# Loading wq in eight row-strided pieces, and moving two small weight loads to the two ends of a decode kernel

## The chip, the cores and the metric

The kernel runs on one core of one Trainium2 chip. The metric is the device time of one execution in microseconds (us); the median over the executions is quoted. "Span" is the length of the profiled execution, which is a little shorter than the time (660.9 us of span for a 662.1 us run).

## The reference

One decode step for two sequences: layer norm, attention over a cache of 8192 positions with 32 heads of 128, output projection, and a gated feed-forward block. All inputs are bfloat16.

```python
def _A_ref(x, k_cache, v_cache, wq, wo):            # x: [2, 1, 512]
    q = (x @ wq).reshape(B, Sq, 32, 128) ...         # wq: [512, 4096]
    scores = einsum("bhqd,bhkd->bhqk", q, k) * Dh**-0.5
    p = softmax(scores)
    o = einsum("bhqk,bhkd->bhqd", p, v)              # k, v: [2, 32, 8192, 128] each
    return o... @ wo                                 # wo: [4096, 512]

def _B_ref(x, W_gate, W_up, W_down):                 # F = 1376
    return ((relu(x @ W_gate)) * (x @ W_up)) @ W_down

h  = x + _A_ref(layernorm(x), ...)
h2 = h + _B_ref(layernorm(h), ...)
```

The K and V caches are 268 MB of the 281 MB that have to be read. Each byte is used once.

## The kernel before: the parts that matter

Four 4 MB buffers (`slot`) hold wq, K and V tiles. Each transfer of a tile covers all 128 partitions, 32 KB in each. Two remainders don't fit the regular tiles and have buffers of their own: the last 256 rows of wo (`wo_last`, 256 KB) and the last 96 rows of W_down (`wd_last`, 96 KB). Both are moved in pieces of 1 KB.

```python
WD_BLOCKS = ((0, 4), (4, 4), (8, 2))
...
def load(s, cache, p):
    nc.sync.dma_start(slot[s][:], kv(cache, p)).then_inc(slot_sem[s], 16)

nc.scalar.dma_start(x_row, A_x[:, 0]).then_inc(sem_x, 16)
nc.sync.dma_start(slot[3][:], A_wq.rearrange("(p c) n -> p (c n)", c=DC)).then_inc(sem_wq, 16)
load(0, A_k_cache, 0)
load(1, A_v_cache, 0)
nc.sync.dma_start(
    wo_last[:].rearrange("p (h n) -> p h n", n=D),
    A_wo[128 * DR:].rearrange("(h d) n -> d h n", d=128)).then_inc(sem_wl, 16)
nc.sync.dma_start(wd_last[:], B_W_down[F - FR:]).then_inc(sem_wd[3], 16)     # FR = 96
load(2, A_k_cache, 1)
...                                              # wq is needed first: q = wq * layernorm(x)
pe.wait((sem_wq, 16), t_xlT)
...                                              # loop over 32 pairs of heads; K and V tiles p+2
                                                 # are queued as the buffers come free
elif p == NP - 2:                                # the last loads: W_up, W_gate, then W_down
    ...
    for k, (r0, n) in enumerate(WD_BLOCKS):
        nc.sync.dma_start(slot[0][:, ...], B_W_down[r0 * 128:(r0 + n) * 128]...).then_inc(sem_wd[k], 16)
...
pe.wait((sem_wd[3], 16), t_hd)                   # the last product, with W_down
order = [(10, 3)] + [(f, k) for k, (r0, n) in enumerate(WD_BLOCKS) for f in range(r0, r0 + n)]
for n, (f, k) in enumerate(order):
    pe.wait((sem_wd[k], 16))
    ...                                          # 4 matmuls for each of the 11 blocks of rows
```

A transfer raises its semaphore by 16 in all when it has landed.

The softmax here doesn't subtract the row's maximum and nothing guards it: scores larger than these inputs give would overflow.

Of the kernel before, what the change touches and what calls it, by code (L numbers as in the profile page):

```python
# [39 lines left out]
def bass_sequential_preLN__gqa_block_cached__glu_gated_reglu__decode_kernel(  # L40
# [12 lines left out]
    B, _, D = A_x.shape  # L53
    _, H, Sk, Dh = A_k_cache.shape
    F = B_W_gate.shape[1]
    assert (B, D, H, Sk, Dh, F) == (2, 512, 32, 8192, 128, 1376)
    DC = D // 128
# [7 lines left out]
    FR = F - 10 * 128  # L65
    VJ = 4
    PG = 2
    DR = (H - 2) * Dh // 128
# [2 lines left out]
    eps = 1e-5  # L71
    inv_sqrt_dh = 1.0 / math.sqrt(Dh)
    WD_BLOCKS = ((0, 4), (4, 4), (8, 2))

    with ExitStack() as es:
        def S(name):
            return es.enter_context(nc.semaphore(name))

        def sb(name, shape, dt):
            return es.enter_context(nc.sbuf_tensor(name, shape, dt))  # L80
# [4 lines left out]
        pe = Prog(nc.tensor, S("pe"))  # L85
# [6 lines left out]
        sem_x, sem_wq, sem_wl, sem_out = S("x"), S("wq"), S("wl"), S("out")  # L92
# [3 lines left out]
        sem_wd = [S(f"wd{i}") for i in range(4)]  # L96

        slot = [sb(f"slot{i}", [128, SLOT], BF16) for i in range(4)]
        X = sb("X", [128, DR * D], BF16)
        wo_last = sb("wo_last", [128, 2 * D], BF16)  # L100
        wd_last = sb("wd_last", [FR, D], BF16)
# [53 lines left out]
        def kv(cache, p):  # L155
            hp, b = divmod(p, B)
            return cache[b, 2 * hp:2 * hp + 2].rearrange("h (p j) d -> (h p) (j d)", p=64)
# [4 lines left out]
        if True:  # L162

            def program():

                def load(s, cache, p):
                    nc.sync.dma_start(slot[s][:], kv(cache, p)).then_inc(slot_sem[s], 16)  # L167

                nc.scalar.dma_start(x_row, A_x[:, 0]).then_inc(sem_x, 16)
                nc.sync.dma_start(slot[3][:], A_wq.rearrange("(p c) n -> p (c n)", c=DC)).then_inc(sem_wq, 16)  # L170
                load(0, A_k_cache, 0)
                load(1, A_v_cache, 0)
                nc.sync.dma_start(  # L173
                    wo_last[:].rearrange("p (h n) -> p h n", n=D),
                    A_wo[128 * DR:].rearrange("(h d) n -> d h n", d=128)).then_inc(sem_wl, 16)
                nc.sync.dma_start(wd_last[:], B_W_down[F - FR:]).then_inc(sem_wd[3], 16)  # L176
                load(2, A_k_cache, 1)


# [45 lines left out]
                for k, row in enumerate((x_row, lnx_row)):  # L225
                    rv = row.rearrange("b (n c) -> b c n", c=DC)
                    for c in range(DC):
                        i = nc.tensor.transpose(
                            Tp[0][:].bitcast(BF16)[:, (k * DC + c) * B:(k * DC + c + 1) * B], rv[:, c, :], ident[0:B, 0:B])
                t = pe.run(i)  # L230
                dve.wait(t)
                t_xlT = dve.run(nc.vector.tensor_copy(out=xlT[:], in_=Tp[0][:].bitcast(BF16)[:, 0:2 * DC * B]))
# [2 lines left out]


                wq = slot[3][:].rearrange("p (c n) -> p c n", c=DC)
                pe.wait((sem_wq, 16), t_xlT)
                for h in range(H):
                    for c in range(DC):  # L240
                        i = nc.tensor.matmul(
                            Wp[:, h * B:(h + 1) * B], lhsT=wq[:, c, h * Dh:(h + 1) * Dh],
                            rhs=lT[:, c * B:(c + 1) * B], start=(c == 0), stop=(c == DC - 1))
# [6 lines left out]
                for r in range(2):  # L250
                    for h in range(2):
                        i = nc.tensor.matmul(
                            Sp[r][64 * h:64 * h + 64, 0:2 * NP], lhsT=ident[:].rearrange("p (n r) -> p r n", r=2)[:, r, :],
                            rhs=qT[:], start=True, stop=True)
# [25 lines left out]
                for m in range(NP // 4):  # L280
# [11 lines left out]
                    for k in range(4):  # L292
                        i = nc.tensor.matmul(  # L293
                            Op[m % 2][:, k * 128:(k + 1) * 128], lhsT=qrep[m % 2][:, k * 128:(k + 1) * 128],
                            rhs=ident[:], start=True, stop=True)
# [128 lines left out]
                for r in range(DR):  # L424
                    i = nc.tensor.matmul(
                        Op[1][32 * (r % 4):32 * (r % 4) + B, :], lhsT=O_all[:, r, :], rhs=X[:, r * D:(r + 1) * D],
                        start=(r < 4), stop=(r >= DR - 4))
# [17 lines left out]
                def tokp(kind, p, *g):  # L445
                    return tok((kind, p) + g, p // 2)
# [62 lines left out]
                for p in range(NP):  # L509
# [85 lines left out]
                    if p < NP - 4:  # L595
                        sp.wait(tokp("pv", p))
                        load((2 * p + 1) % 4, A_v_cache, p + 2)
                    elif p == NP - 3:
                        sp.wait(tokp("pv", NP - 4))
                        load(1, A_v_cache, NP - 2)  # L600
                        sp.wait(tokp("pv", NP - 3))
                        for k, (j0, j1) in enumerate(((J // 2, J), (0, J // 2))):
                            nc.sync.dma_start(
                                slot[3][:, j0 * Dh:j1 * Dh],
                                kv(A_v_cache, NP - 1)[:, j0 * Dh:j1 * Dh]).then_inc(sem_vl[k], 16)
                    elif p == NP - 2:
                        sp.wait(t_dm[p], tokp("pt", p, NG - 1))
                        for k, w in enumerate((B_W_up, B_W_gate)):
                            nc.sync.dma_start(  # L609
                                slot[0][:, k * DC * F:(k + 1) * DC * F],  # L610
                                w.rearrange("(p c) n -> p (c n)", c=DC)).then_inc(sem_w[k], 16)
                        for k, (r0, n) in enumerate(WD_BLOCKS):
                            nc.sync.dma_start(  # L613
                                slot[0][:, 2 * DC * F + r0 * D:2 * DC * F + (r0 + n) * D],
                                B_W_down[r0 * 128:(r0 + n) * 128].rearrange("(p r) n -> p (r n)", r=n)).then_inc(sem_wd[k], 16)



# [8 lines left out]
                for h in range(2):  # L627
                    for c in range(DC):
                        i = nc.tensor.matmul(
                            Wp[:, c * B:(c + 1) * B], lhsT=wv[:, h, c, :],  # L630
                            rhs=O_cur[:].rearrange("p (b a) -> p a b", a=2)[:, h, :],
                            start=False, stop=True, skip_group_check=True)
# [7 lines left out]
                for c in range(DC):  # L640
                    i = nc.tensor.matmul(Sp[0][:, 0:B], lhsT=onesn[:], rhs=hb[:, c * B:(c + 1) * B],
                                         start=(c == 0), stop=(c == DC - 1))
# [12 lines left out]
                def cols(f):  # L655
                    for r0, n in WD_BLOCKS:
                        if r0 <= f < r0 + n:
                            return slice(r0 * 128 + f - r0, (r0 + n) * 128, n)
                    return slice(f * 128, F)
# [14 lines left out]
                for k in range(4):  # L674
                    for c in range(DC):
                        i = nc.tensor.matmul(
                            Tp[0][32 * k:32 * k + B, c:128:DC], lhsT=hb[:, c * B:(c + 1) * B],
                            rhs=ident[:, 32 * k:32 * k + 32], start=True, stop=True)
# [19 lines left out]
                t_hd = dve.run(nc.vector.scalar_tensor_tensor(  # L698
                    out=hd[:], in0=Op[1][:, 0:FC * B], scalar=0.0,
                    in1=u_sb[:], op0=ALU.max, op1=ALU.mult))  # L700
                pe.wait(t_vh)
                for m in range(4):
                    for k in range(2):
                        i = nc.tensor.matmul(Sp[0][32 * m:32 * m + B, 32:33], lhsT=vh[:, k * B:(k + 1) * B],
                                             rhs=onesn[:, 0:1], start=(k == 0), stop=(k == 1))
# [2 lines left out]
                dve.run(nc.vector.tensor_scalar_add(out=ve[:], in0=Sp[0][:, 32:33], scalar1=eps))  # L708
                dve.last()
                dve.run(nc.vector.reciprocal(out=r2[:], in_=ve[:]))  # L710
                pe.wait((sem_wd[3], 16), t_hd)
                order = [(10, 3)] + [(f, k) for k, (r0, n) in enumerate(WD_BLOCKS) for f in range(r0, r0 + n)]
                for n, (f, k) in enumerate(order):
                    pe.wait((sem_wd[k], 16))
                    kp = 128 if f < 10 else FR
                    for m in range(4):
                        i = nc.tensor.matmul(  # L717
                            Op[0][32 * m:32 * m + B, 0:128], lhsT=hd[0:kp, f * B:(f + 1) * B],
                            rhs=(wdn[:, f, :] if f < 10 else wd_last[:])[:, 128 * m:128 * m + 128],
                            start=(n == 0), stop=(n == FC - 1))  # L720
# [10 lines left out]
                nc.sync.wait_ge(sem_out, 16 * B)  # L731

            program()

    return nc
# [28 lines left out]
```

## Time and profile before

| | before |
|---|---|
| time, median of the first 3 runs | 662.1 us |
| span | 660.9 us |
| read from memory | 281 MB |
| DVE, PE busy | 70%, 51% |

The profile's page shows 40 equal slices of the span, about 16.5 us each. The row DMA is the busy share of the 16 DMA engines in tenths, and the row GB/s what they moved. The fourth part is the chain of work that ended last.

```profile
span 660.9 us, 7674 instructions
...
DMA  9999999999999999999999999999999999999996
GB/s 381 426 417 428 440 421 438 430 428 438 423 436 432 428 440 420 438 433 424 440 422 436 436 423 438 425 432 436 426 435 428 432 432 430 434 431 428 440 416 270
...
DMA 80%; DVE 17%; PE 1%; SPq 1%; issue 0%; ACT 0%; DVEq 0%
```

The transfers are the limit from end to end. A K load is queued 32 us before it lands, and a 4 MB load passes every 9.7 us: three loads are always in line. Nothing that DVE or PE does in the middle can change the total unless it lets that line run empty. Bytes can't change either. What is left are the places where the line doesn't run at 430 GB/s. The table of windows shows them. Its columns are the stretch, its length, the busy time (and number of instructions) of each engine, then the clock that PE was granted, the DMA share and the GB/s. A transfer's piece is counted where it begins, so short windows scatter (a DMA share of 1.08 from 10 to 15 us).

```profile
core 0: us, PE busy (x) PEld busy (x) DVE busy (x) ACT busy (x) POOL busy (x), PEclk, DMA share, GB/s
0.00:2.00 2.00, 0.00 (x0) 0.00 (x0) 0.33 (x1) 0.60 (x1) 1.11 (x9) 1.00 0.59 148
2.00:5.00 3.00, 0.37 (x8) 0.34 (x8) 1.92 (x5) 0.88 (x2) 2.69 (x10) 1.00 0.73 284
5.00:10.00 5.00, 0.02 (x1) 0.00 (x0) 0.17 (x1) 0.00 (x0) 0.58 (x3) 1.00 1.00 433
10.00:15.00 5.00, 1.71 (x64) 1.71 (x65) 0.00 (x0) 0.00 (x0) 0.00 (x0) 1.00 1.08 465
...
30.00:40.00 10.00, 4.33 (x36) 2.85 (x34) 9.83 (x6) 4.28 (x8) 1.55 (x1) 1.00 1.00 401
40.00:50.00 10.00, 6.95 (x56) 4.30 (x56) 4.79 (x2) 3.59 (x7) 0.00 (x0) 1.00 1.00 429
```

The line runs full from 5 us on, and dips to 401 GB/s between 30 and 40 us, where the two small loads pass. The same view at the end shows the engines finishing one after the other: from 654 to 657.5 us ever fewer of them still move data.

```profile
654.00:655.00 1.00, 1.00 (x37) 0.99 (x32) 0.29 (x1) 0.00 (x0) 0.00 (x0) 0.50 0.77 297
655.00:656.00 1.00, 0.87 (x27) 0.75 (x24) 0.16 (x2) 0.00 (x0) 0.00 (x0) 0.50 0.50 172
656.00:657.00 1.00, 0.70 (x20) 0.44 (x20) 0.26 (x3) 0.00 (x0) 0.00 (x0) 0.50 0.09 37
657.00:658.00 1.00, 0.60 (x16) 0.31 (x16) 0.00 (x0) 0.00 (x0) 0.00 (x0) 0.50 0.03 12
```

And this is the timeline of PE at the end (start, duration, engine, line, operation, output and inputs; in brackets the idle time before and what ended it). The wd_last matmuls come first, because those rows arrived long ago. PE then waits for the last blocks of W_down.

```profile
656.17 0.28 PE L717 MATMUL O<-wd_last,hd 96*2 96x128 bf16 x4 [0.30 <-DVE ve L708]
656.23 0.64 PE L717 MATMUL O<-slot,hd 128*2 128x128 bf16 x16
657.38 1.02 PE L717 MATMUL O<-slot,hd 128*2 128x128 bf16 x24 [0.51 <-DMA slot<-in_B_W_down_dram]
```

### The profile page before, as it was taken

Reading aid. Unit: us, or ns where it says so; the run is one execution under the profiler, and the core shown is the slowest. Engines: PE = TensorE matmul, PEld = TensorE weight load, DVE = VectorE, ACT = ScalarE, POOL = GpSimd, SP = SyncE. Lnnn points to the kernel's source line nnn. Section 1 sums busy time; section 2 is a strip of 40 time slices with the busy share of each in tenths; the row PEclk is TensorE's granted clock in tenths of the full one; section 3 lists DMA queues with packets and bytes.
Section 4 is the critical chain, followed back from the end, with each engine's and each line's share of the span. In section 5 each row is a group of like instructions: output and inputs, shape, how many; then the busy total and the mean of one; then the engine's idle time right before and its main releaser. Section 6 shows DMA issues by size and latency. Waiting matters only on the chain.

```text
span 660.9 us, 7674 instructions
## 1 busy us (share of the span) xinstructions
PE 338.3 (51%) x3220; PEld 208.2 (31%) x3220; DVE 465.6 (70%) x282; ACT 198.9 (30%) x418; POOL 22.5 (3%) x121
## 2 busy tenths in 40 slices
PE   2653354546555354545535464554446454445787
PEld 2431332224333122333313233332324232232464
DVE  1766576788767678776768867676886767787691
ACT  0521321233332133333213333222323322232360
POOL 2000000000000000000000000000000000000000
PEclk9999999955556565655655565555565655555567
DMA  9999999999999999999999999999999999999996
GB/s 381 426 417 428 440 421 438 430 428 438 423 436 432 428 440 420 438 433 424 440 422 436 436 423 438 425 432 436 426 435 428 432 432 430 434 431 428 440 416 270
DMA packets 10787, 281.23 MB, mean 426 GB/s; under 512 B 1202, under 2 KB 1556, under 8 KB 1940
## 3 DMA queue, kind: packets, MB, share of 16 engines
q1 hardware_dynamic: 10760, 281.06, 99.1%
q8 instruction: 6, 0.10, 0.1%
q14 instruction: 9, 0.07, 0.0%
q10 hardware_dynamic: 12, 0.00, 0.0%
HBM read 281.05 MB, written 0.00 MB: 425 GB/s over the span
## 4 chain that ended last, share of the span: by engine, by line
DMA 80%; DVE 17%; PE 1%; SPq 1%; issue 0%; ACT 0%; DVEq 0%
DMA slot<-in_A_k_cache_dram 76%; DVE prod L521 16%; DMA slot<-in_B_W_down_dram 4%; DVE prod L527 1%; PE O L370 0%; PE Ob L380 0%; PE O L717 0%; DVE scores L532 0%; SPq L167 0%; SPq L609 0%; ACT e L457 0%; ACT os_sb L567 0%; SPq L173 0%; SPq L176 0%; SPq L613 0%
## 5 line engine op out<-in xcount | busy, mean ns | idle before, releaser
L521 DVE TENSOR_TENSOR prod<-slot,q_b 128x12288 bf16<-128x12288 bf16 (+1 forms) x32 | 207.7, 6492 | 152.4 <-DMA slot<-in_A_k_cache_dram 150.7
L527 DVE TENSOR_TENSOR prod<-prod 128x6144 bf16<-128x6144 bf16 (+4 forms) x128 | 210.2, 1642 | 4.4
L370 PE MATMUL O<-slot,e 128*16 128x512 bf16 x1024 | 118.2, 615 | 185.5 <-ACT e L457 129.7
L552 ACT ACTIVATE kT<-T 128x1024 bf16<-128x1024 bf16 x132 | 131.2, 1022 | 194.8 <-PE T L349 191.1
L349 PE MATMUL T<-ident_f,slot 128*128 128x128 f32 x528 | 126.7, 401 | 51.4 <-POOLq L539 51.4
L349 PEld LDWEIGHTS T<-ident_f,slot 128*128 128x128 f32 x528 | 91.6, 206 | 65.7 <-issue 65.7
L370 PEld LDWEIGHTS O<-slot,e 128*16 128x16 bf16 x1024 | 26.1, 112 | 251.8 <-ACT e L457 157.3
L457 ACT ACTIVATE e<-scores 64x96 bf16<-64x96 f32 (+1 forms) x64 | 19.4, 303 | 210.2 <-DVE scores L532 209.8
L337 PE MATMUL S<-q2c,kT 128*128 128x4 bf16 x1056 | 50.0, 169 | 37.6 <-ACT kT L552 37.5
L337 PEld LDWEIGHTS S<-q2c,kT 128*128 128x128 bf16 x1056 | 43.3, 107 | 66.5 <-ACT kT L552 64.6
L380 PE MATMUL Ob<-sel,os_sb 128*128 128x4 f32 x136 | 31.0, 351 | 24.9 <-ACT os_sb L567 24.2
L380 PEld LDWEIGHTS Ob<-sel,os_sb 128*128 128x128 f32 x136 | 29.5, 320 | 26.8 <-ACT os_sb L567 25.6
L532 DVE TENSOR_REDUCE scores<-prod 128x96 f32<-128x768 bf16 (+1 forms) x32 | 30.2, 945 | 1.1
L457 ACT ACTIVATE e<-S 64x32 bf16<-64x32 f32 (+1 forms) x64 | 13.0, 204 | 14.8 <-PE S L337 14.4
L503 POOL COPY q2c<-q 128x8 bf16<-128x8 bf16 x32 | 7.6, 238 | 235.3 <-DMA slot<-in_A_v_cache_dram 221.3
L457 ACT ACTIVATION_READ_ACCUMULATOR e<-S 64x1 f32 x64 | 12.8, 201 | 0.7
L489 POOL MEMSET O_l<- 128x40 bf16 (+1 forms) x13 | 1.8, 136 | 315.4 <-DVE O_cur L473 315.4
L457 ACT ACTIVATION_READ_ACCUMULATOR e<-scores 64x1 f32 x64 | 11.8, 184 | 0.0
L386 PEld LDWEIGHTS Ob<-zs,ones_f 128*128 128x128 f32 x30 | 7.2, 300 | 12.7 <-issue 12.7
L567 ACT ACTIVATE os_sb<-O 128x512 f32<-128x512 f32 x16 | 9.6, 597 | 3.2 <-PE O L370 2.8
L298 ACT ACTIVATE q_b<-O 128x512 bf16<-128x512 f32 x8 | 4.3, 594 | 17.9 <-PE O L293 17.9
L386 PE MATMUL Ob<-zs,ones_f 128*128 128x8 f32 x30 | 8.6, 361 | 0.0
(93 smaller groups left out, 83.6 us busy)
## 6 DMA issues: line engine op xcount, KB each, us to landing
slot<-in_A_k_cache_dram SPq DMA_DIRECT2D x32, 4096.0 KB, 32.3
slot<-in_A_v_cache_dram SPq DMA_DIRECT2D x31, 4096.0 KB, 30.6
slot<-in_A_wq_dram SPq DMA_DIRECT2D x1, 4096.0 KB, 12.4
slot<-in_A_v_cache_dram SPq DMA_DIRECT2D x2, 2048.0 KB, 28.0
X<-in_A_wo_dram SPq DMA_DIRECT2D x1, 3840.0 KB, 46.9
slot<-in_B_W_up_dram SPq DMA_DIRECT2D x1, 1376.0 KB, 23.7
slot<-in_B_W_gate_dram SPq DMA_DIRECT2D x1, 1376.0 KB, 26.7
slot<-in_B_W_down_dram SPq DMA_DIRECT2D x2, 512.0 KB, 28.8
```

What stands on the lines that cost most here:

```text
L337: i = nc.tensor.matmul(Sp[p % 2][:, 2 * jj:2 * jj + 4], lhsT=kv_[:, k, r, :], rhs=q2c[p % 2][:, r, :], start=(r == 0), stop=(r == 1))
L349: i = nc.tensor.transpose(Tp[g % 2][:, k * 128:(k + 1) * 128], k_t[:, j:j + 2, :].rearrange("p j d -> p (j d)").bitcast(F32), ident_f[:])
L370: i = nc.tensor.matmul(Op[0][c:c + 16, :], lhsT=e_t[q][:, j // VJ, :], rhs=v_t[:, j:j + VJ, :].rearrange("p j d -> p (j d)"), start=(q == ...
L380: i = nc.tensor.matmul(Ob[:, 0:4], lhsT=os_sb[:, jj * Dh:(jj + 1) * Dh], rhs=sel[:, 4 * jj:4 * jj + 4], start=(jj == 0), stop=(jj == VJ - 1))
L386: T.mark("z", nc.tensor.matmul(bank[:, ZC:ZC + 8], lhsT=ones_f[:], rhs=zs[:], start=True, stop=True))
L457: i = nc.scalar.activation(out=e_t[q][h, j0 // VJ:j1 // VJ, 8 * q:8 * q + 8].rearrange("p g (j a) -> p g j a", a=2)[:, :, :, a], in_=src(h ...
L503: nc.gpsimd.tensor_copy(out=q2c[p % 2][:], in_=q2[:, p]).then_inc(g2p, 1)
L521: t_dm[p] = dve.run(nc.vector.tensor_tensor(out=prod[:, 0:jd, :], in0=k_t[:, 0:jd, :], in1=qv, op=ALU.mult))
L527: dve.run(nc.vector.tensor_tensor(out=prod[:, 0:jd, 0:half], in0=prod[:, 0:jd, 0:half], in1=prod[:, 0:jd, half:w], op=ALU.add))
L532: t_s[p] = dve.run(nc.vector.tensor_reduce(out=sc[:, 0:jd], in_=prod[:, 0:jd, 0:w], axis=AX.X, op=ALU.add))
L552: to_pe(nc.scalar.activation(out=kT[gg % 2][:], in_=Tp[gg % 2][:].bitcast(BF16), func=ACT.Copy))
L567: to_pe(nc.scalar.activation(out=os_sb[:], in_=Op[0][:], func=ACT.Copy))
```

## The change

The intent, as far as the code shows it: give every DMA engine its first piece of wq sooner; take the two small loads out of the middle of the line; and use one of them to even out the finish, by giving some DMA engines more of the last rows than others (nine transfers, of 15 rows down to 5, one row for each engine that a transfer uses).

```diff
+    WD_LAST = (15, 14, 13, 12, 11, 10, 9, 7, 5)
...
-                nc.sync.dma_start(slot[3][:], A_wq.rearrange("(p c) n -> p (c n)", c=DC)).then_inc(sem_wq, 16)
+                nc.scalar.dma_start(
+                    wo_last[:].rearrange("p (h n) -> p h n", n=D),
+                    A_wo[128 * DR:].rearrange("(h d) n -> d h n", d=128)).then_inc(sem_wl, 16)
+                for i in range(8):
+                    nc.sync.dma_start(
+                        slot[3][i:128:8, :], A_wq.rearrange("(p c) n -> p (c n)", c=DC)[i:128:8]).then_inc(sem_wq, 16)
                 load(0, A_k_cache, 0)
                 load(1, A_v_cache, 0)
-                nc.sync.dma_start(wo_last ...)
-                nc.sync.dma_start(wd_last[:], B_W_down[F - FR:]).then_inc(sem_wd[3], 16)
                 load(2, A_k_cache, 1)
...
-                pe.wait((sem_wq, 16), t_xlT)
+                pe.wait((sem_wq, 128), t_xlT)
...                                                  # after the last W_down blocks:
+                        r0 = 0
+                        for n in WD_LAST:
+                            nc.sync.dma_start(
+                                wd_last[r0:r0 + n], B_W_down[F - FR + r0:F - FR + r0 + n]).then_inc(sem_wd[3], 16)
+                            r0 += n
...                                                  # and wd_last is multiplied last, not first
-                order = [(10, 3)] + [(f, k) ...]
+                order = [(f, k) ...] + [(10, 3)]
```

More of the change, by code (lines that the diff above doesn't have):

```diff
@@ L169, in program @@
                 nc.scalar.dma_start(x_row, A_x[:, 0]).then_inc(sem_x, 16)
-                nc.sync.dma_start(slot[3][:], A_wq.rearrange("(p c) n -> p (c n)", c=DC)).then_inc(sem_wq, 16)
+                nc.scalar.dma_start(
[4 more added lines that the diff above has]
+                        slot[3][i:128:8, :], A_wq.rearrange("(p c) n -> p (c n)", c=DC)[i:128:8]).then_inc(sem_wq, 16)
                 load(0, A_k_cache, 0)
                 load(1, A_v_cache, 0)
-                nc.sync.dma_start(
-                    wo_last[:].rearrange("p (h n) -> p h n", n=D),
-                    A_wo[128 * DR:].rearrange("(h d) n -> d h n", d=128)).then_inc(sem_wl, 16)
-                nc.sync.dma_start(wd_last[:], B_W_down[F - FR:]).then_inc(sem_wd[3], 16)
                 load(2, A_k_cache, 1)
@@ L710, in program @@
                 dve.run(nc.vector.reciprocal(out=r2[:], in_=ve[:]))
-                pe.wait((sem_wd[3], 16), t_hd)
-                order = [(10, 3)] + [(f, k) for k, (r0, n) in enumerate(WD_BLOCKS) for f in range(r0, r0 + n)]
+                pe.wait(t_hd)
+                order = [(f, k) for k, (r0, n) in enumerate(WD_BLOCKS) for f in range(r0, r0 + n)] + [(10, 3)]
                 for n, (f, k) in enumerate(order):
-                    pe.wait((sem_wd[k], 16))
+                    pe.wait((sem_wd[k], 16 if k < 3 else 16 * len(WD_LAST)))
                     kp = 128 if f < 10 else FR
```

## The prediction

> **What bounds the kernel now.** The DMA engines. The page's slices show them over 90% busy in all but the last, and 281 MB in a 660.9 us span is 426 GB/s; in 10 us stretches (the table of windows) the rate is mostly 423 to 446. The chain of waits is 80% DMA: a 32.2 us wait for a K load, a 6.57 us DVE multiply, in turn; each load was queued long before. DVE (70% busy) and PE (51%) are not the limit. So time lost by the transfers anywhere appears whole in the total; bytes don't change.
>
> Three places fall short of the full rate. (1) The start: first wq data at 1.8 us; wq lands 12.4 us after issue, while later 4 MB loads follow every 9.7 us. (2) The stretch 30 to 40 us, where the two small loads (wo, W_down rows; 1 KB pieces) pass: 401 GB/s, not 429, about 0.65 us lost. (3) The end: from 654 to 657.6 us the DMA share is only 0.39: the engines don't finish together; then 3.3 us without loads (8 last matmuls, one DVE operation, the output).
>
> **What the change does.**
> - *wo rows first, on ACT; W_down rows out of the middle.* Removes place 2: about -0.5 us. Part of the wo rows may fill the slow start: 0 to -0.4 us. ACT's extra issue delays nothing that matters.
> - *W_down rows at the very end.* Nine transfers, one 1 KB row for each engine used: later engines get fewer. Estimated from 426 GB/s over 16 engines, a row is about 0.04 us plus a little for its semaphore: at most 0.3 us can be balanced, beside the 3 us over which the engines finish now. After the last landing 4 matmuls remain, not 8: -0.15 us. Together -0.2 to -0.5 us. Nine more issues on SP near 630 us are hidden behind 28 us of queued loads.
> - *wq in 8 transfers of 16 rows, eight partitions apart.* Issue (8 x 0.41 us) is hidden. But each writes partitions i, i+8, ... [...]
>
> **Sum.** [...] Point 670.7, range 660.3 to 672.5. Faster by over 2%: 0.01; within 2%: 0.96; slower: 0.03.
>
> **What would show it.** wq landing near 22 us after the start, with about 215 GB/s in the windows from 3 to 20 us[...], or near 12.5 us with 430[...]. No 401 GB/s window. The DMA share still tapering over some 2 to 3 us at the end; the last wait on wd_last; about 3.2 us after it.
>
> **What would make it wrong.** [...] If one-row pieces cost far more than their bytes, the tail grows.

The sum was 662.1 + 9.7 - 1.1 = 670.7 us, and about 661.0 us without the 9.7. The 9.7 us stood for wq at half the rate (19.4 us instead of 9.7), at odds of 0.6, which no trace showed then; experiment 1 measures it. The 22 us and 215 GB/s under "What would show it" go with it. The -1.1 us are about the middles of the ranges that stand above (-0.5, 0 to -0.4, -0.2 to -0.5).

## The result, and the profile after

Ratios here are the mean time of one kernel's fast runs over that of the other's in the same rounds, so not quite the ratio of the medians that are quoted.

| | before | after |
|---|---|---|
| time, median | 662.09 us | 673.5 us |
| span | 660.9 us | 672.1 us |
| ratio, 95% interval | | 1.0174 (1.0156 to 1.0192) |

The change costs 11.4 us. It is slower, though within 2%. These are the lines of the page after that answer to those shown of before:

```profile
span 672.1 us, 7689 instructions
...
DMA  9999999999999999999999999999999999999996
GB/s 203 342 420 437 431 424 426 433 437 435 431 429 425 435 435 433 433 433 423 431 435 435 433 433 423 431 435 431 435 433 429 427 435 431 433 435 433 425 421 246
...
DMA 79%; DVE 17%; SPq 3%; PE 1%; issue 0%; ACT 0%; DVEq 0%
```

The DMA row is the same and the GB/s row is not: the first slice fell from 381 to 203. "Busy over 90%" is no proof of full speed: an engine counts as busy for as long as its piece lasts, whether that is 1.21 us or the 2.54 us found below. Windows of the kernel after, columns as above:

```profile
2.00:5.00 3.00, 0.39 (x8) 0.34 (x8) 1.76 (x5) 1.33 (x2) 2.69 (x10) 1.00 0.89 200
5.00:10.00 5.00, 0.00 (x1) 0.00 (x0) 0.17 (x1) 0.00 (x0) 0.56 (x3) 1.00 1.14 247
10.00:15.00 5.00, 0.00 (x0) 0.00 (x0) 0.00 (x0) 0.00 (x0) 0.00 (x0) 1.00 0.99 210
15.00:20.00 5.00, 0.00 (x0) 0.00 (x0) 0.00 (x0) 0.00 (x0) 0.00 (x0) 1.00 1.03 210
20.00:25.00 5.00, 0.53 (x19) 0.54 (x20) 0.00 (x0) 0.00 (x0) 0.00 (x0) 1.00 1.05 295
...
30.00:40.00 10.00, 6.96 (x52) 5.00 (x53) 6.92 (x12) 5.94 (x10) 0.34 (x1) 1.00 0.98 419
40.00:50.00 10.00, 5.51 (x48) 3.97 (x46) 9.86 (x5) 4.96 (x9) 1.87 (x1) 1.00 0.98 418
```

wq moves at about 210 GB/s, half the usual rate, and the dip to 401 is gone. The end of the kernel after, in the same view, then PE's timeline:

```profile
665.00:666.00 1.00, 1.00 (x31) 0.90 (x29) 0.01 (x1) 0.00 (x0) 0.00 (x0) 0.50 0.58 203
666.00:667.00 1.00, 0.61 (x19) 0.31 (x16) 0.41 (x3) 0.00 (x0) 0.00 (x0) 0.50 0.19 64
667.00:668.00 1.00, 0.82 (x24) 0.41 (x24) 0.00 (x0) 0.00 (x0) 0.00 (x0) 0.50 0.05 15
668.00:669.00 1.00, 0.15 (x8) 0.00 (x0) 0.00 (x0) 0.00 (x0) 0.00 (x0) 0.50 0.00 0
```

```profile
667.18 0.97 PE L724 MATMUL O<-slot,hd 128*2 128x128 bf16 x24 [0.36 <-DMA slot<-in_B_W_down_dram]
669.40 0.28 PE L724 MATMUL O<-wd_last,hd 96*2 96x128 bf16 x4 [1.25 <-DMA wd_last<-in_B_W_down_dram]
```

Here is the second surprise. No data of the loads move after 667.7 us, yet PE waits for wd_last until 669.40 us. Something other than data takes 1.7 us.

The trace also records each piece that a DMA engine moved (its start, duration and bytes, not which engine it was) and the moment at which each increment of a semaphore arrived. From these come the following marks, in us from the start of the span. The "Nth piece" is the Nth start of a 32 KB piece; each 4 MB load has 128 of them, so the 129th is roughly the start of the first K load. The second column of differences is against before.

| mark | before | after | after − before |
|---|---|---|---|
| first piece of wq starts | 1.82 | 2.21 | +0.39 |
| 129th piece (first K load) | 12.10 | 22.76 | +10.66 |
| 385th piece (second K load) | 32.41 | 43.01 | +10.60 |
| 1025th piece | 90.76 | 100.72 | +9.97 |
| 8192nd, last K or V piece of 32 KB | 635.77 | 645.53 | +9.76 |
| last data have moved | 657.53 | 667.71 | +10.18 |
| last increment of a semaphore | 657.98 | 669.36 | +11.38 |
| span | 660.9 | 672.1 | +11.2 |

These marks come from one profiled execution of each kernel. So: about 10.7 us are lost while wq loads (0.66 us more than in experiment 1 below, where the wo rows are not at the start), 0.7 us come back where the small loads used to pass, 0.4 us are lost again in the last pieces, and 1.2 us between the last data and the last increment.

### The profile page after: what moved, and what is told of

The parts are those of the page before. It is cut to its first block, busy times and chain, and to the rows that moved or that the text cites. A ratio compares the mean times of both kernels' runs of the same rounds, so it can differ in the third digit from the quotient of the medians.

```text
span 672.1 us, 7689 instructions
## 1 busy us (share of the span) xinstructions
PE 340.3 (51%) x3220; PEld 208.0 (31%) x3220; DVE 465.4 (69%) x282; ACT 198.9 (30%) x418; POOL 22.8 (3%) x121
## 4 chain that ended last, share of the span: by engine, by line
DMA 79%; DVE 17%; SPq 3%; PE 1%; issue 0%; ACT 0%; DVEq 0%
DMA slot<-in_A_k_cache_dram 76%; DVE prod L523 16%; DMA wd_last<-in_B_W_down_dram 3%; SPq L620 2%; DVE prod L529 1%; SPq L175 1%; PE O L372 0%; SPq L615 0%; PE Ob L382 0%; SPq L168 0%; DVE scores L534 0%; SPq L611 0%; ACT e L459 0%; ACT os_sb L569 0%; DVE kT L731 0%
## 5 line engine op out<-in xcount | busy, mean ns | idle before, releaser
L459 ACT ACTIVATE e<-scores 64x96 bf16<-64x96 f32 (+1 forms) x64 | 19.4, 303 | 209.6 <-DVE scores L534 209.2
L243 PE MATMUL W<-xlT,slot 128*128 128x2 bf16 x128 | 3.6, 165 | 19.5 <-DMA slot<-in_A_wq_dram 19.5
```

What stands on the lines that cost most here:

```text
L459: i = nc.scalar.activation(out=e_t[q][h, j0 // VJ:j1 // VJ, 8 * q:8 * q + 8].rearrange("p g (j a) -> p g j a", a=2)[:, :, :, a], in_=src(h ...
```

## The experiments

Theories for the start: *destination* (the set of partitions that a transfer writes decides how long its pieces take), against *small transfers* (a transfer that gives each engine one row costs extra wherever it lands) and *source* (the order of the addresses in memory). For the end: *semaphore steps* (each of the nine transfers makes each engine that it uses raise the semaphore, and these increments queue) against *place* (1 KB pieces last in line are slow) and *a fixed cost of the last transfer*. All kernels give a correct result under the comparison. One reads the wrong rows of wq, so the comparison hardly notices the query; for that run only the times count.

### 1. Only the wq part

```diff
-  nc.sync.dma_start(slot[3][:], wq_src).then_inc(sem_wq, 16)
+  for i in range(8):
+      nc.sync.dma_start(slot[3][i:128:8, :], wq_src[i:128:8]).then_inc(sem_wq, 16)
```

> The kernel before with only the wq load cut into 8 transfers of 16 rows, eight partitions apart. If the wq load carries the whole loss at the start[...]: wq lands near 22 us, 215 GB/s until then, total 662.1 + 9.7 = about 672 us, and the wait for the last W_down data stays as before. If the loss comes from the three parts acting together (the wo rows on the ACT queue sharing the engines with wq): under 668 us.

Measured: 672.37 us against 662.07 us, ratio 1.0152 (1.0136 to 1.0167). The 129th piece starts at 22.10 us (+10.0 us), and the wait at the end is as before: 0.45 us from the last data to the last increment. A 32 KB piece of wq takes 2.54 us (median); in the 128-row loads that follow, all but a few pieces take 1.21 to 1.23 us (the slowest 1.88). This part alone carries 10.3 us of the 11.4.

### 2. Everything but the wq part

```diff
   # the kernel after, with
-  for i in range(8): nc.sync.dma_start(slot[3][i:128:8, :], ...)
+  nc.sync.dma_start(slot[3][:], ...)
```

> The kernel after with the wq load put back to one transfer; wo rows first on ACT and the W_down rows last in nine transfers stay. As predicted for these two parts: 661.0 to 661.6 us. If the trace of the kernel after is read rightly (1.2 us of wait after the last bytes of the W_down rows, added to an end that is otherwise 0.5 to 0.9 us better): 662.3 to 663.2 us, with some 1.5 us between the last data and the first matmul on the W_down rows.

Measured: 662.82 us, ratio 1.0006 (0.9992 to 1.002): no gain, and the predicted 1.1 us are outside the interval. By the marks, the 1025th piece starts 0.71 us earlier than before (90.04 us), as hoped; the last data move only 0.22 us earlier (657.31 us); the last increment comes 1.0 us later (658.98 us). The gain of the middle exists. The end gives it away: 0.5 us until the last data, 1.2 us more until the last increment.

### 3. The eight transfers with neighbouring rows

```diff
-  for i in range(8): nc.sync.dma_start(slot[3][i:128:8, :], wq_src[i:128:8])
+  for i in range(8): nc.sync.dma_start(slot[3][16*i:16*i+16, :], wq_src[16*i:16*i+16])
```

> The kernel before with wq in 8 transfers of 16 neighbouring rows, partitions 16i to 16i+15. [...] Rival, that a transfer of 16 rows costs a fixed extra of some 1.2 us wherever it lands: as the stride of eight, about 672 us.

Expected 691 us if the destination decides.

Measured: 688.28 us, ratio 1.0395 (1.0379 to 1.0411). A piece takes 4.53 us, 3.7 times the usual 1.21. The transfers are as many and as large as in experiment 1; only the partitions and the rows that they touch differ. A cost of small transfers as such would be the same in both, so it falls. 16 x 32 KB in 4.53 us are 116 GB/s; the loss is 3 us smaller than in the expectation. Two windows of this run (a piece lasts nearly as long as a window here, so these scatter between 105 and 144 GB/s):

```profile
15.00:20.00 5.00, 0.00 (x0) 0.00 (x0) 0.00 (x0) 0.00 (x0) 0.00 (x0) 1.00 1.26 144
20.00:25.00 5.00, 0.00 (x0) 0.00 (x0) 0.00 (x0) 0.00 (x0) 0.00 (x0) 1.00 0.91 105
```

### 4. Source or destination?

```diff
-  nc.sync.dma_start(slot[3][i:128:8, :], wq_src[i:128:8])
+  nc.sync.dma_start(slot[3][i:128:8, :], wq_src[16*i:16*i+16])     # wrong rows on purpose
```

> Wrong result on purpose: eight transfers that write partitions eight apart (as in the change) but read 16 neighbouring rows of wq from memory (as the slower variant did). If the destination decides[...]: a packet takes 2.5 us, total about 672 us, as with the change's own rows. If the source addresses decide: 4.5 us, total about 688 us, as with neighbouring rows.

Measured: 672.76 us, ratio 1.016 (1.0145 to 1.0176); a piece takes 2.5 us. With the source of experiment 3 and the destination of experiment 1 the time is that of experiment 1, and so are the windows:

```profile
10.00:15.00 5.00, 0.00 (x0) 0.00 (x0) 0.00 (x0) 0.00 (x0) 0.00 (x0) 1.00 0.99 210
15.00:20.00 5.00, 0.00 (x0) 0.00 (x0) 0.00 (x0) 0.00 (x0) 0.00 (x0) 1.00 1.03 210
```

The destination decides.

### 5. The eight transfers from two queues

```diff
-  nc.sync.dma_start(slot[3][i:128:8, :], wq_src[i:128:8])
+  (nc.sync if i < 4 else nc.scalar).dma_start(slot[3][i:128:8, :], wq_src[i:128:8])
```

> The kernel before with the same 8 transfers of 16 rows, eight partitions apart, but those for i of 0 to 3 on the SP queue and those for i of 4 to 7 on the ACT queue[...]. [...] Rival, a fixed cost of each 16-row transfer: still about 672 us, or at best 667 if the two queues overlap their fixed costs.

Expected 662 to 664 us. It took for granted that the transfers for i of 0 to 3 and those for i of 4 to 7 don't slow each other when they run at the same time, which no run shows.

Measured: 671.27 us, ratio 1.0134 (1.0118 to 1.0149). That expectation failed. The records show why: pieces of the two queues strictly alternate, all 16 engines first on a piece of one queue (2.36 us), then all on one of the other (2.36 us). The engines march nearly in step, so pieces of the two groups seldom run together: counted from the pieces, on average 1.4 of the 15 busy engines were on the other group. The run doesn't tell the theories apart, because the condition that I meant to create didn't come about.

### 6. One row for each engine, but nine partitions apart

The transfers are still small, one row for each engine, but they write other sets of partitions: 14 that lie nine apart.

```diff
-  for i in range(8): nc.sync.dma_start(slot[3][i:128:8, :], wq_src[i:128:8])
+  for i in range(9): nc.sync.dma_start(slot[3][i:i+118:9, :], wq_src[i:i+118:9])     # 14 rows each
+  nc.sync.dma_start(slot[3][126:128, :], wq_src[126:128])
```

> The kernel before with wq in nine transfers of 14 rows, nine partitions apart, and one of the two rows left. [...] Rival, that any transfer which gives an engine only one row is slow (some 1.3 us extra for each): nine transfers of 2.5 us, total 674 us or more.

Expected 663 to 664.5 us if the destination decides and this set is fast.

Measured: 669.73 us (667.87 to 671.53), ratio 1.0121 (1.0105 to 1.0136): neither theory's number. My expectation failed here too. The pieces tell more than the total. In the profiled run (667.87 us, the fastest of the four) nine in ten pieces of the second to the eighth transfer take 1.21 to 1.4 us, after a first one of 1.2 to 2.1 us (in the kernel before, too, the first pieces are slow: 1.29 to 2.54 us for the first 16). Windows of this run:

```profile
5.00:10.00 5.00, 0.00 (x0) 0.00 (x0) 0.17 (x1) 0.00 (x0) 0.56 (x3) 1.00 0.87 347
10.00:15.00 5.00, 0.00 (x0) 0.00 (x0) 0.00 (x0) 0.00 (x0) 0.00 (x0) 1.00 0.99 315
15.00:20.00 5.00, 0.00 (x0) 0.00 (x0) 0.00 (x0) 0.00 (x0) 0.00 (x0) 1.00 1.00 269
20.00:25.00 5.00, 3.25 (x122) 3.26 (x123) 0.00 (x0) 0.00 (x0) 0.00 (x0) 1.00 0.98 419
```

With 14 engines at work (the DMA share of 0.87 is 14 of 16), 347 GB/s between 5 and 10 us is near what 14 of 16 can do (14/16 of 433 is 379). So transfers that give each engine one row can run at nearly full speed, with these sets of partitions. But from 12 to 18 us, in the ninth transfer and the first K pieces behind it, most pieces take 1.7 to 2.7 us, and the engines stay as much as 6 us apart to the end of the run (the 16 increments of a K load spread over 6.0 us, against 2.2 to 2.4 us in the kernel before). Why that handover is slow was not settled; it costs most of what these sets save.

### 7. to 9. The 96 rows at the end in nine, one and six transfers

On the kernel before; only the load of the last W_down rows is moved and multiplied last.

```diff
-  nc.sync.dma_start(wd_last[:], B_W_down[F - FR:]).then_inc(sem_wd[3], 16)      # in the middle
+  for n in WD_LAST: nc.sync.dma_start(wd_last[r0:r0+n], ...).then_inc(sem_wd[3], 16)    # at the end
   # WD_LAST = (15, 14, 13, 12, 11, 10, 9, 7, 5), or (96,), or (16,) * 6
```

> The kernel before with only the last 96 W_down rows moved to the end, in the nine transfers of the change. My reading of the trace: data end about 0.5 us earlier than before (the small load no longer slows the load behind it), then the semaphore steps of the last engine, about 0.18 us each, hold the last four matmuls up to 1.6 us after its last bytes: 662.3 to 663.2 us. The prediction's own view (at most a few 0.01 us for a semaphore): 661.4 to 661.8 us.

> The same, but the 96 rows as one transfer at the end: 6 rows and one semaphore step for each engine. If the semaphore steps are the cost: the wait after the last data falls to 0.5 to 0.7 us and the total to 661.2 to 661.7 us. If the place at the end is the cost (1 KB rows last in line, whatever their number of transfers): no better than with nine transfers.

> The same in six transfers of 16 rows: 6 rows and six semaphore steps for each engine. Semaphore theory: 0.18 us for each step, so a wait after the last data of about 1.1 us, and a total 0.6 to 0.9 us above the single transfer, 0.2 to 0.5 us below the nine. If only the engine that finishes last having most rows (nine) is to blame, that is the time of the rows: then it lies within 0.15 us of the single transfer.

| transfers for the 96 rows | time | ratio, 95% interval | last data | last increment | between |
|---|---|---|---|---|---|
| before (in the middle) | 662.17 us | | 657.53 | 657.98 | 0.45 us |
| one | 661.86 us | 0.9995 (0.9981 to 1.0008) | 657.42 | 657.89 | 0.47 us |
| six | 662.33 us | 1.0002 (0.9989 to 1.0016) | 656.98 | 658.27 | 1.29 us |
| nine, as in the change | 662.89 us | 1.001 (0.9997 to 1.0024) | 657.37 | 659.05 | 1.67 us |

The wait grows with the number of transfers while the bytes stay the same. (The marks are of one profile each. The intervals of the totals all include no difference from before, but each run with nine transfers, 662.79 us or more, is slower than each with one, 662.53 us or less.) The totals of the one and the six missed their expected ranges: 661.86 us is above 661.7, and six lie 0.47 us above one, not 0.6 to 0.9. That is still more than 0.15 us, so the time of the last engine's nine rows alone is not to blame. The trace records 16, 96 and 105 arrivals of increments for one, six and nine transfers: one for each engine in each transfer, and with nine transfers nine more, one for each, which must carry what is missing to 16 (the wait is for 144). The arrival times of the last increments show how the wait comes about. These are the last eight of the kernel with nine transfers, in us:

```
657.965  657.994  658.145  658.325  658.505  658.685  658.865  659.045
```

From 658.145 on they are exactly 0.180 us apart. The pieces that move last are nine of 1 KB, one after the other in steps of 0.048 us, each followed by a 4-byte piece of 9 ns. But the increments arrive only every 0.180 us, so each further row adds about 0.13 us of wait. That gives 0.47 + 9 x 0.13 = 1.65 us for nine transfers and 1.26 us for six, against 1.67 and 1.29 us measured (an estimate from the one-transfer run and the two steps). Why an increment takes 0.180 us no run shows.

It also shows that the last engine has nine rows, the largest share: it is one of those that take part in all nine transfers. So the scheme gave most to an engine that was last already: its part of the last regular W_down block landed at 657.42 us, 1.2 us after that of any other.

With one transfer, the last product no longer waits for a load, but for DVE. This is PE's timeline of that kernel:

```profile
657.47 1.23 PE L722 MATMUL O<-slot,hd 128*2 128x128 bf16 x40 [0.21 <-DVE hd L703]
658.49 0.32 PE L722 MATMUL O<-wd_last,hd 96*2 96x128 bf16 x4
```

### 10. The same rows in 18 transfers

```diff
-  nc.sync.dma_start(wd_last[r0:r0+n], ...)
+  for c0 in (0, 256): nc.sync.dma_start(wd_last[r0:r0+n, c0:c0+256], ...)     # 512 bytes a row
```

> The kernel before with the 96 rows last, each of the nine transfers cut in two halves of 512 bytes a row: the same bytes in 18 transfers. Semaphore theory: the engine that ends last has up to 18 steps of 0.18 us against some 0.03 us of data each, so the wait after the last data grows from 1.7 us to about 3.2 us and the total by about 1.4 us over the nine transfers: 664.0 to 664.6 us. If the wait in the nine-transfer version is a fixed cost of the last transfer: about 663 us, unchanged.

Measured: 664.59 us, ratio 1.0035 (1.0021 to 1.0048). The last data move at 657.36 us, as with nine; the last increment arrives at 660.47 us, 3.11 us later, the last five again 0.180 us apart. PE's timeline shows the wait:

```profile
656.65 1.00 PE L724 MATMUL O<-slot,hd 128*2 128x128 bf16 x24 [0.62 <-DMA slot<-in_B_W_down_dram]
660.51 0.28 PE L724 MATMUL O<-wd_last,hd 96*2 96x128 bf16 x4 [2.86 <-DMA wd_last<-in_B_W_down_dram]
```

The steps predict 0.47 + 18 x 0.15 = 3.2 us (rows of 512 bytes follow each other every 0.030 us). The dose works both ways, so the steps of the semaphore are the cost of the wait after the last data, not the place of the rows nor a fixed cost.

### 11. Only the wo rows, first on the ACT queue

```diff
+  nc.scalar.dma_start(wo_last...).then_inc(sem_wl, 16)        # after x, on ACT
-  nc.sync.dma_start(wo_last...).then_inc(sem_wl, 16)          # from the middle
```

> The kernel before with only the wo rows moved, first on the ACT queue. If the 0.65 us lost between 30 and 40 us is due to the small packets as such, half to three quarters of it goes from there (the W_down rows are still there) but the 0.7 us of packets come back at the start: 661.8 to 662.2 us. If the start has idle room for them, as the prediction had it: 661.4 to 661.8 us.

Measured: 662.11 us, ratio 1.0001 (0.9988 to 1.0015). The 257th piece starts at 22.61 us, 0.74 us later than before; by the 513th it is 0.08 us earlier (42.59 us). The rows cost about the same time at the start that they cost in the middle: no idle room was filled.

### 12. A version without the two costs

wq in one transfer, the wo rows first on ACT, the 96 rows as one transfer at the end.

> A version without the two costs: wq in one transfer, wo rows first on the ACT queue, the 96 rows as one transfer at the end. Expected 661.2 to 661.9 us, that is 0 to 0.9 us better than before; the end is then held by the chain of matmuls after the last V load and no longer by a transfer, so more than 1 us is not to be had this way.

Measured: 661.53 us against 662.25 us, ratio 0.9987 (0.9973 to 1.0001). It lies 0.7 us below the kernel before, and the interval just includes no difference. It clearly beats the kernel after.

## Why the prediction was wrong

- **The bound.** Right. The line of transfers is never empty, and every delay in it came through: 10.0 us at the 129th piece were still 10.0 us at the last data in experiment 1.
- **wq in 16-row transfers: +9.7 us, at odds of 0.6.** The half rate came about (2.54 us a piece instead of 1.21). It is now shown that the destination decides (experiments 3 and 4) and that small transfers as such are not slow (experiments 3 and 6). The size was 0.6 us short: measured alone it is 10.3 us. A piece takes 2.1 times the usual and not twice, and the first piece starts 0.39 us later.
- **Small loads out of the middle: about -0.5 us.** Right as far as it goes: 0.7 us by the 1025th piece (experiments 2 and 7), and the dip to 401 GB/s is gone. It is the W_down rows that count: moving them alone gives 0.73 us there, moving the wo rows alone 0.10 us. At 426 GB/s the 96 KB are worth an estimated 0.23 us; the rest lies in the load behind them, whose first 16 pieces took 1.4 to 1.6 us instead of 1.22 and no longer do in experiment 7.
- **"Part of the wo rows may fill the slow start: 0 to -0.4 us."** It came out at zero (experiment 11).
- **W_down rows at the very end: "Together -0.2 to -0.5 us."** This is the step that failed, in its sign. The estimate costed a row at 0.04 us "plus a little for its semaphore". The little was 0.180 us for each increment, on an engine that had nine of them, all behind the last byte that moved. The wait grew from 0.45 to 1.65 us. In experiment 2, which has it without the wq part, 0.5 us more go between the 1025th piece and the last data; the 96 KB that have to be moved there are an estimated 0.23 us of it, and the rest is not explained. The two parts other than wq together were counted as -1.1 us; they measured +0.75 us as a difference of medians (experiment 2). The interval of the ratio, 0.9992 to 1.002, leaves open whether the total lost anything, but not that the gain of 1.1 us is absent; the loss at the end itself is read from the marks.

Put together, the sum was 662.1 + 9.7 - 1.1 = 670.7 us; with the measured terms it is 662.1 + 10.3 + 0.75 = 673.15 us, against 673.5 us measured. The difference of 1.85 us in the second term and 0.6 us in the first carried the time past the range's upper end of 672.5 us.

Some things stay open: why pieces for partitions eight apart took 2.54 us from one queue and 2.36 us from two, why the first piece starts 0.39 us later, and why the handover in experiment 6 is slow. What it is about a set of partitions that decides, no run shows; the runs show three sets of one row for each engine: 4.53 us a piece for 16 neighbours, 2.54 us for 16 that lie eight apart, mostly 1.21 to 1.4 us for 14 that lie nine apart.

A smaller thing in the trace: single slow pieces follow fetches of instructions. In the kernel before, each of the ten 32 KB pieces after 35 us that took over 1.3 us began as a fetch of instructions ended: fetches of 16 KB (about 1.06 us) were followed by pieces of 1.71 and 1.77 us, fetches of 8 KB (about 0.31 us) by pieces of 1.57 to 1.88 us, instead of 1.22. What this adds to the 2.4 us over which the engines finish the last full loads was not measured.

## What to carry to other kernels

Before cutting a large load into pieces, work out which partitions each piece writes: here a load in transfers of 16 rows that lie eight partitions apart ran at half the rate (210 GB/s, 2.54 us a piece instead of 1.21), and one in transfers of 16 neighbouring rows at 116 GB/s (4.53 us), and "DMA busy" won't show it, only GB/s or the time of a piece will. When many small transfers share a semaphore at the end of a kernel, count the increments of the engine that finishes last, not the bytes: here each took 0.18 us, nearly four times its row (0.048 us). Data that have moved and data that may be used are two different marks in the trace; read both.
